# Two groups of three score banks for ScalarE with the third lent to VectorE, and one ring of 24 exp tiles

## Chip, cores and metric

The kernel runs on one core of a Trainium2 chip. The metric is the device time of one execution in microseconds, as the median of several runs; the profile is of one further execution. The profile's engines are PE (TensorE), PEld (its weight loads), ACT (ScalarE), DVE (VectorE), POOL (GpSimd) and SP (the engine that issues most DMAs).

## What is computed

Two independent halves whose outputs stand side by side in the last dimension: an SSM convolution (A) and an attention with 32 query heads on one shared key and value head (B). Everything is bf16 outside; S = 2048, D = 640, head size 20.

```python
# A: diagonal complex state space
Lam_bar = exp(dt * Lam);  B_bar = ((Lam_bar - 1) / Lam)[:, None] * Bmat
Bu = einsum("bld,pd->blp", x + 0j, B_bar)
h_t = Lam_bar * h_{t-1} + Bu_t
y = 2 * einsum("blp,dp->bld", h, Cmat).real + x * Dskip
# B: attention, 32 query heads on one key and one value head
q = (x @ wq) as 32 heads of 20;  k = x @ wk;  v = x @ wv
p = softmax(q k^T * 20 ** -0.5);  o = (p v) @ wo
out = concatenate([y, o], -1)
```

## The kernel before

**Work.** The attention is cut into 32 blocks (4 stretches of 512 queries, 8 groups of 4 heads). A block has 64 score tiles of 128 keys by 512 queries (16 key chunks, 4 heads), so there are 2048 in all. A score tile is one TensorE matmul into a PSUM bank (`score`, L1131). Its exponential is made in one of two ways:

- by ScalarE, for a *group* of adjacent banks at once: one ACTIVATE with Exp reads the group from PSUM (SC) and writes bf16 tiles to PR (L1117);
- by VectorE, for one tile: a TENSOR_SCALAR from its bank into an integer tile DR (`fill_d`, L1236), whose bits read as bf16 are an approximate exponential. It is sharpened by three shifted copies, made from DR to DR by VectorE in ones or pairs (`copy_source`) or by GpSimd in pairs (`pool_source`), each with its own scaled values VS. So one such tile needs four PV matmuls.

PV matmuls multiply exp tiles by the values and accumulate, four heads at a time, in one bank (`pv_source`, L1336). When all 64 tiles of a block are in, VectorE evacuates this bank (pvsb, L1385), and later steps divide by the sums and project with WO. SSM work (20 units of 10 VectorE steps or more, and 20 output steps), the query projections and the output projections are *tasks*: each takes a free bank from `misc` when its due number of tiles has been reached (`manager`).

**PSUM.** The 8 banks are: two exp groups, SC0 with three banks and SC1 with two (`CHUNKS`), two `misc` banks, and one bank for PV. VectorE's score tiles take a free misc bank.

**Exp buffers.** PR has 8 places (`NPS`), each of three tiles. Exp number k takes place k mod 8, and may not start before the PV matmuls of the last user of this place are done (the gate at L1120).

**Order.** The order of each engine's instructions is fixed when the program is built. A planner (`Schedule`, L40) keeps a model of the five engines with a duration for each step, and at each moment gives a free engine the ready step of the least `prio`. The steps that matter here: a group's fill 0, a block's PV evacuation 0.3, VectorE score tiles 0.5, SSM products out of PSUM 0.52, the other SSM steps 3, PV matmuls 2.0, or 0.9 when an exp place that is needed is still unread (`tight`). SSM steps that are late get 0.4 and a little, one step in each PAUSE. Semaphore waits are then derived from reads and writes. On the chip each engine does its instructions in this order, and each waits for the others.

**The fill.** `attention` alternates between the groups. A fill (`fill`, L1094) is one TensorE step: it scores the group's tiles, and up to `4 - n` VectorE tiles into free misc banks. It waits for the exp that last read the group. `want_d` and `can_d` decide on VectorE tiles: a share of at most 0.25, four of the 18 DR buffers free, a free bank.

Of the kernel before, what the change touches and what calls it, by code (L numbers as in the profile page):

```python
# [9 lines left out]
ALU = mybir.AluOpType  # L10
# [29 lines left out]
class Schedule:  # L40
# [12 lines left out]

    PAUSE = 1000.0
    LOCK = 60.0
# [102 lines left out]
    def pick(self, eng):  # L158
        urgent = None
        t = self.t  # L160
        cands = self.pending[eng]
        for src in self.sources[eng]:
            extra = src()
            if extra is not None:
                cands = cands + [extra]
        can, held = [], []
        for op in cands:
            r = self.ready(op)
            if r is None:
                continue  # L170
            if op.gate is not None and not op.gate():
                if op.due is not None and r <= t + 1e-6 and (urgent is None or op.due < urgent):
                    urgent = op.due
                continue
            if r <= t + 1e-6:
                if op.port:
                    if self.port_free["pool" if eng == "dve" else "dve"] > t + 1e-6:
                        if eng == "dve":
                            held.append(op)
                        continue  # L180
                    if eng == "pool" and self.port_wanted:
                        continue
                can.append(op)
            elif op.prio <= self.URGENT and (urgent is None or r < urgent):
                urgent = r
        best = key = None
        for op in can:
            p, dur = op.prio, op.dur
            if op.late and t >= self.late_from:
                p = 0.4 + 0.02 * p  # L190
            if eng == "pe" and op.mode != self.mode:
                dur += self.SWITCH
                if p > self.URGENT and self.stay():
                    p += self.STAY
            if urgent is not None and p > self.URGENT and t + dur > urgent + self.slack.get(eng, 1e9):
                continue
            if best is None or (p, op.seq) < key:
                best, key = op, (p, op.seq)
        if eng == "dve":
            self.port_wanted = any(best is None or op.prio < best.prio for op in held)  # L200
        return best
# [185 lines left out]
class Holder:  # L387


    def __init__(self, index):  # L390
        self.index = index
        self.left = 0
        self.users = []
        self.taken = False
        self.waits = False

# [10 lines left out]
class Build:  # L407
    CHUNKS = (3, 2)
    MISC = 2
    NPS = 8  # L410
    NOP = 7
# [58 lines left out]
    def alloc(self, o):  # L470
# [15 lines left out]
        self.WOt = sb(o, "WOt", [128, 640], BF16)  # L486
        self.PR = sb(o, "PR", [128, self.NPS, max(self.CHUNKS), 512], BF16)
        self.tab = sb(o, "tab", [128, 2, NC, 512], BF16)
# [114 lines left out]
    def program(self):  # L603
# [9 lines left out]
        self.state_op = {}  # L613
        self.hold = [Holder(i) for i in range(self.NPS)]
        self.nhold = 0
        self.dhold = [Holder(i) for i in range(self.NDS)]
# [26 lines left out]
    def warm_source(self):  # L643

        if self.started or self.s.t > 40000.0:
            return None
        p = self
        return Op("pe", [self.mm(self.pvbank.ap, p.PR[:, 0, 0, 0:128], p.PR[:, 0, 0, :], True, True)], 260.0, prio=9,
                  load=512.0, deps=[self.zero_op], reads=["PR0"], writes=[self.pvbank.key], hook=self.warm_last)
# [26 lines left out]
    def constants(self):  # L676
        self.zero_op = self.dve(lambda e: e.memset(self.PR[:, 0, 0, :], 0.0), 200, writes=["PR0"], prio=0.1)
        p = self
# [238 lines left out]
    def qt_task(self, bank):  # L917

        p = self
        prev = self.pe(self.four(bank, [p.VZ[:]] * 4, p.PR[:, 0, 0, :], True, False), self.mmt(512),  # L920
                       deps=[self.c_op["VZ"], self.zero_op] + bank.last, prio=0.95, mode="C", reads=["VZ", "PR0"], writes=[bank.key])
# [110 lines left out]
    def attention(self):  # L1032
# [8 lines left out]
        self.slot_last = [[op for b in bs for op in b.last] for _, bs in self.slots]  # L1041
        self.pv_gate = list(self.pvbank.last)
        while self.tile_n < NTILE:
            i = k % len(self.slots)
            yield lambda: (fill is None or fill.start is not None) and all(o.start is not None
                                                                          for o in self.slot_last[i])
            if self.tile_n >= NTILE:
                break
            n = min(self.CHUNKS[i], NTILE - self.tile_n)
            near = [self.act_block()]  # L1050
# [13 lines left out]
        for i in (k % 2, (k + 1) % 2):  # L1064
            yield lambda: fill.start is not None and all(o.start is not None for o in self.slot_last[i])
            for bank in self.slots[i][1]:
                bank.last, bank.busy = list(self.slot_last[i]), False
                self.misc.append(bank)
                self.free_banks.append(bank)

    MARGIN = 650.0

    def fill_now(self, op, i, n):

        s = self.s
        other = self.slot_last[1 - i]
        if len(other) != 1 or other[0].start is None or not self.d_count:
            return True
# [15 lines left out]
    def fill(self, op, i):  # L1094
        p = self
        t, banks = self.slots[i]
        n = min(self.CHUNKS[i], NTILE - self.tile_n)
        h = self.hold[self.nhold % self.NPS]
        self.nhold += 1
        extra, used = [], set()  # L1100
        while len(extra) < 4 - n and self.want_d(len(extra)):
            m = self.take_d(used)
            if m is None:
                break
            extra.append(m)
        tiles = [self.take_tile(used) for _ in range(n)]
        ents = []
        for x, m in enumerate(tiles):
            b, kc, j = self.score(op, m, t[:, 512 * x:512 * x + 512], banks[x])
            ents.append((b, kc, j, p.PR[:, h.index, x, :]))  # L1110
        for m in extra:
# [3 lines left out]
        op.load = 128.0 * len(op.fns)  # L1115
        dst = p.PR[:, h.index, 0:n, :]
        ex = self.act(lambda e: e.activation(dst, t[:, 0:512 * n], ACT.Exp, scale=1.0 / UNIT),  # L1117
                      0.8333 * 512 * n + 64, table="exp",
                      deps=[op], reads=[b.key for b in banks[:n]], writes=[f"PR{h.index}"], prio=0.5,
                      gate=lambda: not h.taken or (h.left == 0 and self.s.done(h.users)))  # L1120

        def on_start(_):
            h.taken, h.left, h.users, h.waits = True, n, [], False
        h.waits = True
        ex.hook = on_start
        self.slot_last[i] = [ex]
        for b, kc, j, rhs in ents:
            self.pvq[b][j].append((p.VP[:, kc, 0:32], kc, rhs, f"PR{h.index}", ex, h, "VP"))
            self.pv_filled[b] += 1

    def score(self, op, m, out, bank):  # L1131
# [65 lines left out]

    def want_d(self, taken=0):
        s = self.s
        if self.tile_n >= NTILE - 8 or self.d_count + taken + 1 > self.SHARE * (self.tile_n - 16):  # L1200
            return False
        if len(self.d_banks()) <= taken:
            return False
        return len(self.d_free()) > taken + len(self.SHIFTS) - 1

# [12 lines left out]
    ALONE, TASK, PV = 1.9, 0.95, 2.0  # L1218
    EV, P1, COPY, COPY1 = 0.52, 0.5, 0.56, 0.6
    CLOSE, PVEV = 0.3, 0.3  # L1220

# [13 lines left out]

    def fill_d(self, op, m):  # L1236

        p = self
        bank = self.d_banks()[0]
        self.take([bank])  # L1240
        h = self.d_free()[0]
# [5 lines left out]
        first = self.dve(self.ts(p.DR[:, h.index, :], bank.ap, 16256.0, 0.0, ALU.add, ALU.max), 663, deps=[op],  # L1247
                         reads=[bank.key], writes=[key], prio=self.P1)
        self.s.spawn(self.d_give(bank, first))
        self.d_open.append([h, first, list(range(1, n)), b, kc, j])  # L1250
        self.d_left[b, j] += n - 1
        self.pv_entry(b, kc, j, 0, h, first)
        self.pv_filled[b] += 1

    def pv_entry(self, b, kc, j, k, h, op):
# [80 lines left out]
    def pv_source(self):  # L1336
# [18 lines left out]
        left = sum(len(x) for x in q)  # L1355
        h = self.hold[self.nhold % self.NPS]
        tight = h.taken and h.left > 0 or any(x.waits and x.left > 0 for x in self.hold)
        if len(group) < 4 and not tight and not (complete and left < 12 and len(group) == sum(1 for x in q if x)):
            return None
        prio = 0.9 if tight else self.PV  # L1360
        return Op("pe", [], self.mmt(512, len(group)), prio=prio, mode="C", load=128.0 * len(group), hook=lambda op: self.pv(op, b, group))
# [166 lines left out]
    def finish(self, prev, rows, bank, ops, end=None):  # L1528
# [7 lines left out]
        else:  # L1536
            key, st = f"PR{end}", self.PR[:, end, 0, :]
        last = self.stage_dma.get(key)
# [13 lines left out]
    def ssm_scalars(self):  # L1552
# [128 lines left out]
        for c in range(NC):  # L1681
            self.diag_op = self.dve(self.ts(p.diagD[:, c, :], p.ident[:], sc[:, DSK, c:c + 1], None, ALU.mult), 160,
                                    deps=[sc_op, self.c_op["ident"]], reads=["sc", "ident"], writes=["diagD"], prio=3)
# [271 lines left out]
```

## Time and profile before

| | us |
|---|---|
| median of 5 runs | 768.7 (768.47 to 769.35) |
| profiled execution: whole, span | 769.16, 767.4 |
| ScalarE, VectorE, TensorE, GpSimd busy | 743.0, 666.4, 717.6, 436.4 |
| exps: first start, end of the last | 23.8, 755.8 |

In a group's row of the profile, the columns are the line, engine, operation, output and input tile with shapes, count, then busy us and the mean ns of one, then the idle time before them with what ended it. Buffer numbers are left out, so all PR places read PR, the two exp groups SC, and misc and PV banks MB. [...] A row of waits reads: who waited for whom, us in total, times, the longest. L581, L585, L595 and L600 are helpers that many steps share, so tiles tell them apart: SC<-QT,KT or MB<-QT,KT is a score, MB<-PR,VP and MB<-DR,VS are PV, MB<-xaT,BT and MB<-CT are SSM, DR<-MB is a VectorE score tile, DR<-DR its copies.

### The profile page before, as it was taken

To read this page: it belongs to the slowest core of one execution; us is meant where nothing else is said; L and a number is where in the kernel's file an instruction comes from. 1 tells how busy PE (TensorE), PEld (TensorE's weight loads), DVE (VectorE), ACT (ScalarE), POOL (GpSimd) and SP (SyncE) were. 2 spreads that over 40 slices of the span, in tenths; PEclk is the share of its full clock that TensorE was granted. 3 is DMA by queue.
4 is the path that set the end of the run, shared out by engine and by line. 5 is a ranking of instruction groups with operands and counts; after the bars stand their busy time and mean duration, and the time that the engine had idled before them with its cause. 6 is when DMAs were issued, how large, how long until landed. Compare 5 with 4: busy or idle time off the path is not lost.

```text
span 767.4 us, 24010 instructions
## 1 busy us (share of the span) xinstructions
PE 717.6 (94%) x10217; PEld 239.2 (31%) x10217; DVE 666.4 (87%) x1239; ACT 743.0 (97%) x668; POOL 436.4 (57%) x454
## 2 busy tenths in 40 slices
PE   9999999998999999999889999999989999999997
PEld 3432223222223233332233322223322332233223
DVE  6989999889899898999899888998988889984786
ACT  5899999999999999999999999999999999999994
POOL 4765666365556444466646575446556556556961
PEclk9999999999999999999999999999999999999999
DMA  9935200100001111020001111120000000001001
GB/s 192 137 89 100 62 24 8 41 20 9 9 18 25 31 30 57 30 48 14 7 12 32 35 31 34 46 50 17 11 18 15 25 25 22 16 11 28 25 10 42
DMA packets 61770, 27.87 MB, mean 36 GB/s; under 512 B 44936, under 2 KB 61664, under 8 KB 61664
## 3 DMA queue, kind: packets, MB, share of 16 engines
q1 hardware_dynamic: 60332, 26.20, 14.6%
q8 instruction: 81, 1.33, 0.7%
q10 hardware_dynamic: 1332, 0.13, 0.2%
q14 instruction: 25, 0.20, 0.1%
HBM read 8.31 MB, written 8.12 MB: 21 GB/s over the span
## 4 chain that ended last, share of the span: by engine, by line
ACT 81%; PE 15%; DVE 2%; SPq 1%; issue 0%; DMA 0%; POOL 0%; DVEq 0%; POOLq 0%
ACT PR L1117 81%; PE MB L581 5%; PE MB L585 5%; PE SC L585 4%; PE SC L581 1%; SPq L570 0%; DMA xaT<-in_A_x_dram 0%; POOL fr L600 0%; DVE QP L956 0%; DVE mab L814 0%; DVE fr L600 0%; DVE DR L600 0%; ACT tab L1622 0%; DVE prod L599 0%; DVE QT L600 0%
## 5 line engine op out<-in xcount | busy, mean ns | idle before, releaser
L1117 ACT ACTIVATE PR<-SC 128x1536 bf16<-128x1536 f32 (+1 forms) x642 | 726.6, 1374 | 5.6 <-PE MB L585 3.3
L595 POOL TENSOR_TENSOR DR<-DR,step 128x512 int32<-128x512 int32 x406 | 415.4, 1047 | 299.9 <-DVE DR L600 146.2
L600 DVE TENSOR_SCALAR DR<-MB 128x512 int16<-128x512 f32 x444 | 295.7, 684 | 64.2 <-PE MB L585 59.1
L585 PE MATMUL SC<-QT,KT 32*128 32x512 bf16 x1604 | 250.5, 384 | 40.0 <-ACT PR L1117 30.2
L585 PE MATMUL MB<-DR,VS 128*32 128x512 bf16 x1776 | 233.4, 384 | 0.4 <-DVE pvsb L1385 0.2
L585 PE MATMUL MB<-PR,VP 128*32 128x512 bf16 x1604 | 220.3, 385 | 0.9 <-DVE pvsb L1385 0.6
L585 PE MATMUL MB<-QT,KT 32*128 32x512 bf16 x444 | 160.3, 384 | 0.4 <-DVE prod L595 0.3
L585 PEld LDWEIGHTS SC<-QT,KT 32*128 32x128 bf16 x1604 | 63.8, 91 | 265.8 <-ACT PR L1117 181.4
L600 DVE TENSOR_SCALAR DR<-DR 128x1024 int16<-128x1024 int16 (+1 forms) x290 | 102.7, 408 | 7.8 <-PE MB L585 6.6
L585 PEld LDWEIGHTS MB<-DR,VS 128*32 128x32 bf16 x1776 | 59.4, 94 | 66.1 <-issue 38.1
L585 PEld LDWEIGHTS MB<-PR,VP 128*32 128x32 bf16 x1604 | 55.9, 94 | 63.2 <-issue 42.9
L581 PE MATMUL MB<-xaT,BT 128*32 128x512 bf16 x800 | 59.3, 382 | 0.3
L595 DVE TENSOR_TENSOR prod<-MB,Z 128x1024 bf16<-128x1024 f32 x40 | 48.6, 1215 | 4.8 <-PE MB L581 4.3
L585 PE MATMUL MB<-KT,VZ 128*32 128x256 bf16 x876 | 48.5, 275 | 0.0
L585 PEld LDWEIGHTS MB<-QT,KT 32*128 32x128 bf16 x444 | 38.1, 91 | 24.1 <-issue 14.8
L1725 DVE TENSOR_TENSOR_SCAN g<-sc,hst,u 128x512 bf16<-128x512 f32 x30 | 39.6, 1326 | 0.0
L595 DVE TENSOR_TENSOR prod<-g,tab 128x1024 bf16<-128x1024 bf16 x40 | 31.4, 786 | 0.0
L581 PE MATMUL MB<-xbT,wqf 128*32 128x512 bf16 x400 | 29.9, 395 | 0.5 <-DVE DR L600 0.2
L581 PE MATMUL MB<-CT,W 128*32 128x512 bf16 (+1 forms) x640 | 29.4, 301 | 0.2 <-DVE DR L600 0.2
L581 PE MATMUL MB<-CT,xbT 128*32 128x512 bf16 (+1 forms) x640 | 28.4, 301 | 0.1
L1542 DVE CAST stg<-MB 128x512 bf16<-128x512 f32 x35 | 24.0, 685 | 5.1 <-PE MB L581 4.7
L581 PE MATMUL MB<-WO,OP 128*32 128x128 bf16 (+1 forms) x580 | 27.1, 293 | 0.2
(137 smaller groups left out, 364.7 us busy)
## 6 DMA issues: line engine op xcount, KB each, us to landing
out_dram<-stg SPq DMA_DIRECT2D x35, 128.0 KB, 1.8
qd<-QP SPq DMA_DIRECT2D x20, 128.0 KB, 1.7
QT<-qd SPq DMA_DIRECT2D x28, 80.0 KB
OP<-pvsb SPq DMA_DIRECT2D x108, 20.0 KB
rdP<-recs SPq DMA_DIRECT2D x108, 20.0 KB
CT<-in_B_x_dram SPq DMA_DIRECT2D x2, 640.0 KB, 5.8
WO<-in_B_wo_dram SPq DMA_DIRECT2D x1, 800.0 KB, 4.7
wqf<-in_B_wq_dram SPq DMA_DIRECT2D x1, 700.0 KB, 5.9
```

Of the source, the lines that this page charges most:

```text
L581: r = e.matmul(out[32 * j:32 * j + 32], lhsT=lhsT[:, 32 * j:32 * j + 32], rhs=rhs, start=start, stop=stop, tile_position=(0, 32 * j), skip ...
L585: return lambda e: e.matmul(out, lhsT=lhsT, rhs=rhs, start=start, stop=stop, **kw)
L595: return lambda e: e.tensor_tensor(out, a, b, op)
L600: return lambda e: e.tensor_scalar(out, a, s1, s2, op0=op0, op1=op1)
L1117: ex = self.act(lambda e: e.activation(dst, t[:, 0:512 * n], ACT.Exp, scale=1.0 / UNIT), 0.8333 * 512 * n + 64, table="exp", deps=[op], re ...
L1542: ev = self.dve(lambda e: e.tensor_copy(st, bank.ap), 620, deps=[prev], reads=[bank.key], writes=[key], prio=self.EV, gate=(lambda: last.e ...
L1725: o = self.dve(lambda e, ri=ri, init=init: e.tensor_tensor_scan(p.g[:, u, ri, :], rdec, p.u[:, ri, :], init, ALU.mult, ALU.add), 1280, por ...
```

## The change

- Both exp groups have three banks, and one misc bank is left. The third banks are lent to `misc` until the first half of the queries is ready (`reclaim`); until then groups are of two tiles.
- In a fill of three, the third bank may hold a VectorE score tile (`want_own`). The exp then covers two tiles, VectorE evacuates the third, and the next fill of the group waits for both. Such a step has priority 0.42 and a due time. VectorE steps without a due time are not started when they would run past the earliest one.
- PR is one ring of 24 tiles, and an exp of two takes two. An exp waits for the PV matmuls of those whose tiles it takes.
- VectorE score tiles are not taken while an SSM unit is over 120 tiles late (`behind`).
- PV matmuls of a complete block have priority 0.9. PAUSE is 500 instead of 1000. One small VectorE step on the diagonal is marked as using the port shared with GpSimd.

```diff
-    PAUSE = 1000.0
+    PAUSE = 500.0
...
+        limit = min((op.due for op in self.pending[eng] if op.due is not None), default=1e18) if eng == "dve" else 1e18
         for op in can:
             p, dur = op.prio, op.dur
+            if op.due is None and t + dur > limit:
+                continue
...
-    CHUNKS = (3, 2)
-    MISC = 2
-    NPS = 8
+    CHUNKS = (3, 3)
+    MISC = 1
+    NPT = 24
...
     def attention(self):
...
+        self.cap = [n - 1 for n in self.CHUNKS]
+        for i in range(len(self.slots)):
+            lent = self.slots[i][1][-1]
+            self.misc.append(lent)
+            self.free_banks.append(lent)
+        s.spawn(self.reclaim())
...
     def fill(self, op, i):
-        n = min(self.CHUNKS[i], NTILE - self.tile_n)
-        h = self.hold[self.nhold % self.NPS]
-        self.nhold += 1
-        extra, used = [], set()
-        while len(extra) < 4 - n and self.want_d(len(extra)):
+        n = min(self.cap[i], NTILE - self.tile_n)
+        extra, used, own = [], set(), None
+        if n == 3 and self.want_own():
+            own = self.take_d(used)
+        if own is not None:
+            n = 2
+        while len(extra) < 4 - self.cap[i] and self.want_d(len(extra), own is not None):
...
         tiles = [self.take_tile(used) for _ in range(n)]
+        h = self.pr_take(n)
...
+        first = [] if own is None else [self.fill_d(op, own, banks[2])]
+        if first:
+            other = self.slot_last[1 - i][0]
+            begin = self.s.t + self.mmt(512, 4) + 200
+            if other.eng == "act":
+                begin = max(begin, other.start + other.dur if other.start is not None else self.s.t + other.dur)
+            first[0].due = begin + 2 * (0.8333 * 1024 + 64) - self.REFILL
...
-                      gate=lambda: not h.taken or (h.left == 0 and self.s.done(h.users)))
+                      gate=lambda: all(x.taken and x.left == 0 and self.s.done(x.users) for x in h.prev))
...
-        self.slot_last[i] = [ex]
+        self.slot_last[i] = [ex] + first
...
+    def reclaim(self):
+        yield lambda: (0, 0) in self.half_op
+        for i in range(len(self.slots)):
+            bank = self.slots[i][1][-1]
+            yield lambda: bank in self.free_banks
+            self.free_banks.remove(bank)
+            self.misc.remove(bank)
+            self.slot_last[i] = self.slot_last[i] + bank.last
+            self.cap[i] = self.CHUNKS[i]
...
+    def pr_next(self, n):
+        return self.pr_at if self.pr_at + n <= self.NPT else 0
+
+    def tight(self):
+        at = self.pr_next(3)
+        return any(x is not None and x.taken and x.left for x in self.owner[at:at + 3]) \
+            or any(x.left for h in self.waiting for x in h.prev)
+
+    WAITING = 2
+    REFILL = 900.0
+
+    def want_own(self):
+        if self.tile_n >= NTILE - 8 or self.d_count + 1 > self.SHARE * (self.tile_n - 16) or self.behind():
+            return False
+        if sum(1 for o in self.firsts if o.start is None) >= self.WAITING:
+            return False
+        self.firsts = [o for o in self.firsts if o.start is None]
+        return len(self.d_free()) > len(self.SHIFTS) - 1
...
+    def behind(self):
+        while self.next_unit < NQB * NC:
+            w = self.w_op.get(divmod(self.next_unit, NC))
+            if w is None or w.start is None:
+                return self.tile_n > self.unit_due[divmod(self.next_unit, NC)] + self.LAG
+            self.next_unit += 1
+        return False
...
     def want_d(self, taken=0, own=0):
...
-        if len(self.d_banks()) <= taken:
+        if len(self.d_banks()) <= taken or self.behind():
...
     def fill_d(self, op, m, bank=None):
+        own = bank is not None
+        if not own:
+            bank = self.d_banks()[0]
+            self.take([bank])
...
-                         reads=[bank.key], writes=[key], prio=self.P1)
-        self.s.spawn(self.d_give(bank, first))
+                         reads=[bank.key], writes=[key], prio=self.P1OWN if own else self.P1)
+        if own:
+            self.firsts.append(first)
+        else:
+            self.s.spawn(self.d_give(bank, first))
...
     def pv_source(self):
-        prio = 0.9 if tight else self.PV
+        prio = 0.9 if tight or complete else self.PV
```

## The prediction

> **What bounds the kernel now.** I read the page's busy shares first, then the chain that ended last, then the groups with shapes kept apart, then ScalarE's own waits and timeline.
>
> ```profile
> PE 717.6 (94%) x10217; PEld 239.2 (31%) x10217; DVE 666.4 (87%) x1239; ACT 743.0 (97%) x668; POOL 436.4 (57%) x454
> ```
> ```profile
> ACT 81%; PE 15%; DVE 2%; SPq 1%; issue 0%; DMA 0%; POOL 0%; DVEq 0%; POOLq 0%
> ```
> ScalarE (ACT) is busy 97% of the span and carries 81% of the chain. TensorE's 94% is no second bound: 876 of its matmuls (MB<-KT,VZ) are fillers issued only when the planner finds it underused. VectorE (DVE) at 87% is the one to watch.
>
> ```profile
> L1117 ACT ACTIVATE PR<-SC 128x1536 bf16<-128x1536 f32 x321 | 509.2, 1586 | 4.0 <-PE MB L585 1.9 <-PE SC L585 1.7
> L1117 ACT ACTIVATE PR<-SC 128x1024 bf16<-128x1024 f32 x320 | 371.8, 1162 | 1.6 <-PE MB L585 1.4
> L600 DVE TENSOR_SCALAR DR<-MB 128x512 int16<-128x512 f32 x444 | 295.7, 684 | 64.2 <-PE MB L585 59.1 <-POOL DR L595 0.2
> ```
> The exps (PR<-SC) are 321 of three tiles and 320 of two; VectorE makes 444 score tiles. The 1586 and 1162 ns overlap the next record: in the trace the middle distance from one exp's start to the next is 1335 ns for three tiles and 906 ns for two, so 429 ns for a tile and 48 ns for each instruction. A VectorE score tile costs 607 ns in the same measure. The exps run from 23.8 us to 755.8 us, 732 us; 321 x 1.335 + 320 x 0.906 + 0.5 for a last single tile are 718.9. Most of the remainder, 14.5 us over all pairs of starts (the rest is the last record's tail), is ScalarE waiting. Two waits stand out:
>
> ```profile
> ACT PR L1117 <- PE MB L585: 3.3, 2, 1.9
> ```
> ```profile
> 328.76 3.75 ACT L1117 ACTIVATE PR<-SC 128x1536 bf16<-128x1536 f32 x3
> 333.89 2.37 ACT L1117 ACTIVATE PR<-SC 128x1024 bf16<-128x1024 f32 x2 [1.37 <-PE MB L585]
> ```
> Here an exp waits not for scores but for a PV matmul (MB<-PR) to free its place in the exp ring. The other waits are late fills, many under 0.3 us. TensorE's weight loads say what a fill waits for:
>
> ```profile
> PEld SC L585 <- ACT PR L1117: 181.4, 410, 1.2
> PEld SC L585 <- DVE DR L600: 44.5, 100, 1.3
> ```
> A fill mostly waits for the exp that frees its banks, but 100 times for a VectorE score tile. The trace gives the loop's slack: a fill can start about 300 ns after the start of the exp running meanwhile, and an exp that came late started 442 ns after its fill. 742 of 906 ns: 164 ns are left.
>
> **The exps.** The changed kernel as built (its instruction order, without times) has 253 exps of three tiles and 414 of two: 1587 tiles against 1604, and 667 instructions against 642. 253 x 1.335 + 414 x 0.906 = 712.9 us against 718.9: **-6.0**. So 17 tiles (7.3 us) go to VectorE, and 25 more instructions at 48 ns give 1.2 us back. [...] The rows show 48 ns back to back, so I keep -6.0.
>
> **The ring.** It held 8 groups, a place of three tiles each: 8 x 1.12 = 9.0 us of exps. Now 24 tiles in a row: 24/2.38 groups x 1.069 = 10.8 us. It is 1.8 us deeper, the waits were 1.37 and 1.90 us, and the PV matmuls of a complete block move up to priority 0.9. I take **-3.2**. Ends: -3.6 (both, by start distances) and 0, if new ones come, since the last PV matmuls of a block still wait for the PV bank's evacuation. Behind the waiting exp stand all later exps; with the wait gone, its fill, already in place, lets it start.
>
> **A VectorE tile in the third bank.** 397 of 461 VectorE score tiles now sit in a ScalarE group (DR<-SC), only 64 elsewhere. The refill of that group then waits for the exp and for this VectorE instruction; queued behind it on TensorE are all PV, SSM and projection matmuls, and ScalarE waits one exp later. In the built order 139 fills name a VectorE instruction issued after the exp as a wait, against 68 before. How much room is there? A score tile's evacuation started at best 430 ns after its fill's start, and a fill that waited for one started about 730 ns after it. With exps of 906 ns the refill is due by 1812 + 164 ns after the last fill of that group, so an evacuation can be 1976 - 730 - 430 = 816 ns late for nothing.
>
> Own tiles come in 74 runs of 1 to 15 on successive two-tile exps. Within the runs I added up the VectorE order with the trace's start distances (score tile 607, pair copy 356, single copy 202, SSM product out of PSUM 1133, scan 1230, casts 600). Between two own tiles stand on average 312 ns of other work, so VectorE is asked for 919 ns per 906 ns exp: full, with no reserve, while over the whole kernel its order sums to 643 us against 622 before. Where the sum runs ahead of the exps by more than 816 ns, the excess is a stall: 7.6 us in 27 runs, or 5.0 without the first five, where which exps have an own tile is least sure. I take 6.3. It replaces 2.5 us of waits of exps behind VectorE score tiles in the old trace (20 late exps). Net **+3.8**. Ends: -2.5 (none stalls, excluded below that because no more of the kind existed) and +18.2 (VectorE 7% slower than the distances, as its 666.4 busy us stand to 622, and only 600 ns of room: 20.7 - 2.5).
>
> **Shorter windows.** Outside the large waits an exp of two lost 15 ns on average to late fills, one of three 7.6 ns. 414 and 253 of them make 8.1 us against 7.3; two thirds of that is not VectorE's: **+0.6**, ends 0 and +3.
>
> **What I cost at nothing.** Holding VectorE tiles back while SSM is late, PAUSE and the diagonal's port flag move VectorE and TensorE work that lies under exps; uncovered, it would show as SSM running past the last exp. In the built order the last SSM output stands 87 score matmuls before the end (91 before), some 30 us, so the cover holds. One misc bank fewer is made up by lending the two third banks until the first query half is ready. No DMA is added, 550 on SP's queue as before; GpSimd's copies go from 406 to 402. The head has the same ScalarE steps in nearly the same order; the first exps are of two tiles, and the start and the end (11.6 us after the last exp, outputs and their DMAs) may each move by 1 us.
>
> **Sum.** -6.0 - 3.2 + 3.8 + 0.6 = -4.8 us. The profiled execution took 769.16 us (span 767.4, 1.8 around it), 0.46 above the median of 768.7. So 764.4 for such an execution, and **763.9 us** as the median.
>
> **Rivals.**
> - *VectorE becomes the bound inside the runs (slower).* For it: 919 ns asked per 906 ns, and a static order, so one 1.2 us product in front of an own tile delays refill and exp. Against it: old own distances are 607 ns where the planner reckons 663, so it leaves slack, and it lets no undated VectorE step start that would overrun a dated score tile. With VectorE 7% slower the stalls are 13.6 us, and 20.7 with 600 ns of room; less 2.5 and with the other terms the kernel ends at 771 to 778, say 774 us. It decides from 11.1 us of such stalls on, 28 ns per own tile.
> - *The exps' gain is given back in full.* Ring waits return, since 1.8 us of depth is about the size of one wait, and own tiles stall by 6.3 us: -6.0 + 3.8 + 0.6 + 1 for the head, about 768.1 us.
> - *The larger gain.* Own tiles never stall, as their due times keep VectorE free: -6.0 - 3.6 - 2.5 = -12.1, less 1 for the end, about 755.6 to 757.5 us.
> - *It does not do what it says* is excluded for the counts: own tiles, the ring and the exps of two are in the built order.
>
> **Chances.** Likeliest, at 763.9 (761 to 767): 0.42. Larger gain, about 757: 0.16. Given back, about 768: 0.14. VectorE-bound, about 774: 0.28. The range of 8 in 10 runs from 756 to 775. About 0.2%, 1.5 us, is what measurement can tell from no change: faster 0.58, same 0.13, slower 0.29.
>
> **What would show it.** Right: two exp groups of 253 and 414, starts 1335 and 906 ns apart; ScalarE's wait for MB matmuls with PR gone or below 0.5 us; ScalarE's idle gaps small, and "SC <- DVE DR" among TensorE's waits above 44.5 us without ScalarE idling more than 10 us. Wrong: rows of ScalarE waiting for SC matmuls, released in turn by DVE DR<-SC, of 10 us or more in the runs of two-tile exps; VectorE busy over 700 us; or a start of the exps after 25 us.

## The result and the profile after

The changed kernel takes 765.85 us (median of 41 runs, 761.77 to 771.96), the kernel before 769.2 us beside it (76 runs, 768.09 to 770.97). The ratio is 0.9961 with a 95% interval of 0.9952 to 0.9970: 3.3 us faster. The prediction was 763.9, that is 4.8 us faster. A second difference was not forecast: the runs of the changed kernel lie 10 us apart, those of the kernel before 3 us.

The profiled execution took 767.64 us (span 765.9). Busy times of the page, then the chain that ended last:

```profile
PE 700.4 (91%) x10231; PEld 232.8 (30%) x10231; DVE 678.7 (89%) x1282; ACT 739.3 (97%) x693; POOL 431.4 (56%) x450
```
```profile
ACT 80%; PE 17%; DVE 1%; issue 1%; DMA 0%; POOL 0%; SPq 0%; DVEq 0%; POOLq 0%
```
ScalarE is still the bound: 97% busy, 80% of the chain. It has 3.7 us less work; VectorE has 12.3 us more, and stays under 700.

The groups with shapes kept apart:

```profile
L1139 ACT ACTIVATE PR<-SC 128x1024 bf16<-128x1024 f32 x414 | 399.1, 1124 | 7.3 <-PE SC L588 5.6 <-PE MB L588 1.0
L1139 ACT ACTIVATE PR<-SC 128x1536 bf16<-128x1536 f32 x253 | 355.1, 1573 | 0.5 <-PE SC L588 0.2
L603 DVE TENSOR_SCALAR DR<-SC 128x512 int16<-128x512 f32 x397 | 264.9, 684 | 37.6 <-PE SC L588 26.3 <-PE MB L588 8.5
```
The counts are those of the built program. In the trace the middle distances between starts are 1330 ns for three tiles and 904 for two, in the kernel before 1331 and 904; the 1335 and 906 of the prediction are a few ns high in both. So the exps alone are about 6 us shorter. The 397 new evacuations of a third bank take what an evacuation of a shared bank took, 684 ns.

ScalarE's waits and TensorE's weight loads that waited:

```profile
ACT PR L1139 <- PE SC L588: 5.8, 12, 1.8
ACT PR L1139 <- PE MB L588: 1.0, 1, 1.0
...
PEld SC L588 <- ACT PR L1139: 195.8, 415, 1.2
...
PEld SC L588 <- DVE DR L603: 51.9, 115, 0.9
```
The two ring waits of 3.3 us have become one of 1.0, and it is a score matmul, not a PV matmul of PR, that releases it. The loads wait 115 times for a VectorE score tile where it was 100, and none of these waits is longer than 0.9 us. What is new is the first row: 5.8 us of exps that wait for scores. The timeline of ScalarE shows where:

```profile
23.69 2.83 ACT L1139 ACTIVATE PR<-SC 128x1024 bf16<-128x1024 f32 x3
28.35 1.02 ACT L1139 ACTIVATE PR<-SC 128x1024 bf16<-128x1024 f32 x1 [1.83 <-PE SC L588]
30.29 1.02 ACT L1139 ACTIVATE PR<-SC 128x1024 bf16<-128x1024 f32 x1 [0.92 <-PE SC L588]
31.80 1.02 ACT L1139 ACTIVATE PR<-SC 128x1024 bf16<-128x1024 f32 x1 [0.49 <-PE SC L588]
33.31 1.02 ACT L1139 ACTIVATE PR<-SC 128x1024 bf16<-128x1024 f32 x1 [0.49 <-PE SC L588]
34.67 5.60 ACT L1139 ACTIVATE PR<-SC 128x1024 bf16<-128x1024 f32 x6 [0.33 <-PE SC L588]
```
Five exps in a row come late within 7 us of the head, 4.1 us in all. The view by stretches shows TensorE there. Its columns are stretch, length, busy us and instructions of TensorE, weight loads, VectorE, ScalarE and GpSimd, then the granted clock, the DMA share and GB/s. First the kernel before:

```profile
25.00:30.00 5.00, 4.69 (x112) 1.84 (x116) 4.76 (x12) 3.48 (x5) 4.51 (x10) 0.66 1.03 129
30.00:35.00 5.00, 4.83 (x67) 1.39 (x63) 4.66 (x10) 5.00 (x5) 4.28 (x10) 1.00 0.73 118
60.00:80.00 20.00, 18.41 (x229) 5.28 (x229) 17.95 (x35) 20.00 (x19) 11.06 (x12) 1.00 0.49 97
```
and the changed kernel:

```profile
25.00:30.00 5.00, 3.08 (x78) 1.10 (x76) 3.43 (x9) 2.54 (x3) 4.51 (x9) 0.70 0.55 92
30.00:35.00 5.00, 5.00 (x42) 1.08 (x40) 3.26 (x9) 3.40 (x4) 4.38 (x11) 0.62 0.23 59
60.00:80.00 20.00, 17.45 (x214) 5.23 (x214) 16.04 (x31) 19.86 (x19) 11.56 (x12) 0.95 0.54 98
```
Both have TensorE at half clock in the head, the kernel before for 3.4 us from 26.3 us on, the changed one for 6.8 us from 27.0 on, and again for 3.4 us at 78.2. From 30 to 35 us TensorE is busy all the time and finishes 42 matmuls where the kernel before finished 67. The stretch at 27.0 us has something in front of it: TensorE stands idle for 1.9 us in the midst of a row of small matmuls for v.

```profile
25.07 0.27 PE L584 MATMUL SC<-wvr,xbT 128*32 128x20 bf16 x15
27.25 0.52 PE L584 MATMUL SC<-wvr,xbT 128*32 128x20 bf16 x45 [1.92 <-issue]
```
"issue" means that the profile shows nothing that TensorE waited for. A gap among these matmuls that nothing shown ends, of 0.4 to 1.9 us, stands in the profiles of all kernels below with two groups of three, except own_light; the kernel before and the two kernels built on it have none. So it comes with the change, but not in every execution: own_light has the same TensorE order in the head, and its profile shows neither the gap nor a half-clock stretch. Its line for 25 to 30 us is

```profile
25.00:30.00 5.00, 5.00 (x116) 1.79 (x114) 4.79 (x14) 5.00 (x6) 4.43 (x10) 1.00 0.73 117
```

From the starts of the exps one can sum what ScalarE lost: each distance to the next exp that is over 40 ns beyond 1335 or 906 ns, sorted by what released the fill behind it. The table has the profiled executions that matter below, in us, with the number of late exps in brackets; the last four columns divide the loss after 40 us.

| kernel | first exp | lost before 40 us | lost after 40 us | behind PV of PR | behind a score tile in a shared bank | behind one in the third bank | behind anything else |
|---|---|---|---|---|---|---|---|
| before | 23.8 | 1.9 | 10.4 | 3.5 (6) | 4.2 (34) | none | 2.7 |
| changed | 23.7 | 4.6 | 13.4 | 0.2 (1) | 1.7 (4) | 5.5 (24) | 6.0 |
| own_light | 23.7 | 0.5 | 12.1 | 0.2 (1) | 1.7 (5) | 3.7 (26) | 6.5 |
| head_fill | 23.8 | 2.1 | 12.1 | 0.2 (1) | 1.5 (3) | 4.8 (24) | 5.6 |
| prod_light | 26.1 | 2.6 | 12.3 | 0.2 (1) | 1.4 (3) | 3.9 (17) | 6.8 |

Of these five, only the executions of the changed kernel and of prod_light have a half-clock stretch between 40 us and the last exp, each one of 3.4 us at 78 us.

Before to after: exps -6.0, losses in the head +2.7, losses later +3.0, distances late by 40 ns or less -0.7, first exp and tail -0.2. That is -1.2 against spans that differ by -1.5.

### The profile page after: what moved, and what is told of

The parts are those of the page before. It is cut to its first block, busy times and chain, and to the rows that moved or that the text cites. A ratio compares the mean times of both kernels' runs of the same rounds, so it can differ in the third digit from the quotient of the medians.

```text
span 765.9 us, 24175 instructions
## 1 busy us (share of the span) xinstructions
PE 700.4 (91%) x10231; PEld 232.8 (30%) x10231; DVE 678.7 (89%) x1282; ACT 739.3 (97%) x693; POOL 431.4 (56%) x450
## 4 chain that ended last, share of the span: by engine, by line
ACT 80%; PE 17%; DVE 1%; issue 1%; DMA 0%; POOL 0%; SPq 0%; DVEq 0%; POOLq 0%
ACT PR L1139 79%; PE MB L588 6%; PE SC L588 5%; PE MB L584 5%; PE SC L584 1%; DMA xaT<-in_A_x_dram 0%; ACT tab L1707 0%; POOL fr L603 0%; ACT PR L1625 0%; DVE fr L603 0%; DVE DR L603 0%; ACT L1713 0%; DVE prod L598 0%; DVE pvsb L1470 0%; DVE mab L818 0%
## 5 line engine op out<-in xcount | busy, mean ns | idle before, releaser
L1139 ACT ACTIVATE PR<-SC 128x1024 bf16<-128x1024 f32 (+1 forms) x667 | 723.0, 1295 | 7.8 <-PE SC L588 5.8
L598 POOL TENSOR_TENSOR DR<-DR,step 128x512 int32<-128x512 int32 x402 | 410.4, 1046 | 302.9 <-DVE DR L603 124.8
L588 PE MATMUL SC<-QT,KT 32*128 32x512 bf16 x1984 | 262.0, 386 | 51.5 <-ACT PR L1139 43.4
L603 DVE TENSOR_SCALAR DR<-SC 128x512 int16<-128x512 f32 x397 | 264.9, 684 | 37.6 <-PE SC L588 26.3
L588 PE MATMUL MB<-PR,VP 128*32 128x512 bf16 x1587 | 213.2, 385 | 1.7 <-ACT PR L1139 1.2
L588 PEld LDWEIGHTS SC<-QT,KT 32*128 32x128 bf16 x1984 | 67.8, 91 | 290.0 <-ACT PR L1139 195.8
L603 DVE TENSOR_SCALAR DR<-DR 128x1024 int16<-128x1024 int16 (+1 forms) x316 | 114.9, 417 | 12.8 <-PE MB L588 9.8
L603 DVE TENSOR_SCALAR DR<-MB 128x512 int16<-128x512 f32 x64 | 43.4, 679 | 2.5 <-PE MB L588 2.3
L1627 DVE CAST stg<-MB 128x512 bf16<-128x512 f32 x35 | 23.8, 679 | 5.3 <-PE MB L584 5.2
L588 PEld LDWEIGHTS MB<-KT,VZ 128*32 128x32 bf16 x840 | 21.4, 96 | 12.6 <-issue 6.2
L1470 DVE CAST pvsb<-MB 128x512 bf16<-128x512 f32 x32 | 21.8, 682 | 3.5 <-PE MB L588 3.3
```

The costliest lines, as they stand in the source:

```text
L588: return lambda e: e.matmul(out, lhsT=lhsT, rhs=rhs, start=start, stop=stop, **kw)
L598: return lambda e: e.tensor_tensor(out, a, b, op)
L603: return lambda e: e.tensor_scalar(out, a, s1, s2, op0=op0, op1=op1)
L1470: ev = self.dve(lambda e: e.tensor_copy(p.pvsb[:, slot, :], bank.ap), 620, deps=[op], reads=[bank.key], writes=[f"pvsb{slot}"], prio=self. ...
L1627: ev = self.dve(lambda e: e.tensor_copy(st, bank.ap), 620, deps=[prev], reads=[bank.key], writes=[key], prio=self.EV, gate=(lambda: last.e ...
```

## The experiments

Two theories of where 1.5 us of the forecast gain went. **VectorE** (A in the expectations): an own tile in the third bank is late because VectorE is full, as the prediction had it. **The clock** (B and C): TensorE falls to half clock after stretches with thin work, and fills come late. The second comes from the runs themselves: each run's record gives a mean granted clock. Over the 41 runs of the changed kernel it lies between 0.985 and 0.999, and a straight line through them falls by 0.66 us per 0.001. At 0.9975, about where the kernel before runs (0.997 or 0.998 in 60 of 64 runs, 0.994 to 0.996 in four), the line gives 763.7 us (within 0.5). The 11 runs at 0.997 or more have a median of 763.9 us. A stretch of 3.4 us at half clock takes 0.0022 off the mean, so 1.5 us by that line. The line alone is no proof: what holds up TensorE could lengthen a run and lower its clock at once. Below, "clock" is the mean over the runs of one kernel. The kernel before took 769.0 to 769.15 us beside each of these kernels.

**own_light.** VectorE's evacuation of an own tile at half size.

```diff
-        first = self.dve(self.ts(p.DR[:, h.index, :], bank.ap, 16256.0, 0.0, ALU.add, ALU.max), 663, deps=[op],
+        w = 256 if own else 512
+        first = self.dve(self.ts(p.DR[:, h.index, 0:w], bank.cols(0, w), 16256.0, 0.0, ALU.add, ALU.max), 663, deps=[op],
```


> The changed kernel with the same instruction order; the VectorE evacuation of a tile in an exp group covers 256 of 512 columns, so that part of the exponentials is left out. Each of the 397 takes some 267 ns less. Theory A (the refill waits for VectorE's own tile, some 5.5 us in the profile after): the changed kernel's 765.9 us falls by 4 to 5.5, to about 761, and the waits of fills for DVE DR<-SC nearly vanish. Rival B (what is given back is lost to stretches in which TensorE's clock is granted at half): it falls by less than 1 us, and the spread of 10 us between runs stays.

Measured: 765.91 us (762.49 to 768.53), ratio 0.9954 (0.9936 to 0.9973), clock 0.994. Nothing changed, though the row shows that the edit took hold:

```profile
L603 DVE TENSOR_SCALAR DR<-SC 128x256 int16<-128x256 f32 x393 | 163.5, 420 | 106.8 <-PE SC L588 87.7 <-PE MB L588 17.6
```
101 us less VectorE work (264.9 to 163.5) brought nothing, and idle time in front of these evacuations rose from 37.6 to 106.8 us. So that VectorE is full is not what costs the time; that theory falls. The exps behind a third bank lose 1.8 us less than in the changed kernel's profile, but no time comes of it; and 15 of the 26 late evacuations here begin after VectorE stood idle until their score came, so the fill was late and not VectorE. The line through these runs gives 763.6 at clock 0.9975, as for the changed kernel.

**keep_more.** More fillers for TensorE.

```diff
-    KEEP = 3500.0
+    KEEP = 5000.0
```


> The changed kernel with the planner's threshold for filler matmuls raised from 3500 to 5000: 2192 fillers in place of 840, exps of 710.7 us by their counts against 712.8. Rival B: the stretches at half clock go, some 1.9 us each and two to three in a mean run; with the exps' 2.1 us the time falls to about 760, and runs differ by less than 3 us. Theory A: only the exps' 2.1 us, 763.8, and the spread stays. If fillers get in the way of fills: over 766.

Measured: 770.63 us (767.67 to 774.62), ratio 1.0013 (0.9996 to 1.0031), clock 0.991. A miss for the clock: 2192 filler matmuls instead of 840 did not remove the half-clock stretches (10.2 us from 27.6 on, 6.8 us at 676). This source gives nothing before a PV block is open, and so nothing in the head. The time is that of the third case, fillers in the way of fills: the line through these runs gives 766.0 us at clock 0.9975 (within 1.2), 2.2 us above the changed kernel. The edit changes the order too, so it cannot tell what the stretches cost.

**ring_alone.** The kernel before with the ring of 24 tiles only.

```diff
-    NPS = 8
+    NPT = 24
...
-        h = self.hold[self.nhold % self.NPS]
-        self.nhold += 1
+        h = self.pr_take(n)
```


> The kernel before with one part of the change alone: the ring of 24 tiles in place of 8 places of three; groups of 3 and 2 as before. By counts the exps come to 720.7 us, 2.2 more than before. Theory A (the ring is worth the 3.6 us that ScalarE waited for it): 769.2 + 2.2 - 3.6 = 767.8, and no wait of an exp for PV matmuls. Rival (those waits move to other places): 771.4.

Measured: 769.8 us (768.81 to 770.97), ratio 1.0005 (0.9997 to 1.0014). This lies between the two cases. Its order has 322 and 321 exps and no single tile at the end, 720.7 us by counts against 718.9 with the single tile: 1.8 us more, not 2.2. So the ring itself gave about 1 us by the medians; in the profiles late exps behind PV of PR fell from 3.5 us (6) to 1.7 (2). Half of the waits stay.

**places_8.** The changed kernel with eight places of three tiles.

```diff
-        self.owner[at:at + n] = [h] * n
-        self.pr_at = at + n
+        self.owner[at:at + 3] = [h] * 3
+        self.pr_at = at + 3
```


> The changed kernel with the ring undone: each exp takes a place of three tiles, 8 places. Exps by counts 710.4 us against 712.8; depth 8 exps of 1.06 us, 8.5 us. Theory A: waits for the ring come back, 3.5 us or more, so 767 us or above. Rival (the ring gives nothing): 763.5.

Measured: 772.26 us (769.18 to 774.75), ratio 1.0036 (1.0022 to 1.0050), clock 0.988. 6.4 us more than the changed kernel, although its exps are 2.4 us shorter by counts: late exps behind PV of PR are back, 2.6 us (7), and part of the rest goes with the lower clock. At clock 0.9975 the line through its runs gives 768.1 us (within 1.5), 4.4 above the changed kernel. With two-tile exps the ring is worth more than in the kernel before, as far as a changed order allows the comparison.

**fill_small.** Each filler cut to one small matmul.

```diff
+        fns = [self.mm(bank.tensor[0:32, bank.off:bank.off + 16], p.VZ[:], p.KT[:, 0:16], False,
+                       False, tile_position=(0, 0), skip_group_check=True)]
         self.n_keep += 1
```


> The changed kernel with every filler cut down: where TensorE gets four 128-column matmuls that add zero to a PV bank while a window has nothing else for it, it now gets one of 16 columns. The order of the instructions on every engine is otherwise that of the changed kernel (252 + 415 three- and two-tile exps or within one of it), nothing of the computation is left out. Theory C (part of what the change should have brought is lost to TensorE's clock, which falls to half for stretches of 3.4 us after stretches with thin TensorE work): more such stretches than the two of the changed kernel's profile before 700 us, a mean granted clock under 0.985, and a median above the changed kernel's 765.9, by about 1.5 us for each stretch more: 768 to 780, with a wider spread. Rival (the fillers only stand in front of the next score tiles, and the clock is no matter): 764 to 766, the late exps released by a score matmul fewer than in the changed kernel.

The matmuls that go have 256 columns each, not 128.

Measured: 771.06 us (767.72 to 775.08), ratio 1.0032 (1.0011 to 1.0053), clock 0.979. 5.2 us slower by taking work away. Of the profile, by stretches:

```profile
120.00:140.00 20.00, 17.57 (x198) 5.57 (x198) 16.65 (x28) 19.33 (x18) 12.81 (x13) 0.91 0.12 32
140.00:160.00 20.00, 16.73 (x187) 5.15 (x179) 18.55 (x37) 18.97 (x18) 7.05 (x7) 0.91 0.04 10
160.00:180.00 20.00, 17.92 (x197) 5.19 (x194) 18.22 (x35) 19.36 (x19) 11.50 (x12) 0.91 0.03 6
```
and of the changed kernel:

```profile
120.00:140.00 20.00, 18.53 (x257) 6.13 (x250) 17.73 (x32) 20.00 (x19) 11.62 (x12) 1.00 0.11 30
140.00:160.00 20.00, 17.07 (x241) 5.61 (x233) 19.04 (x35) 19.93 (x19) 7.90 (x9) 1.00 0.04 11
160.00:180.00 20.00, 17.21 (x230) 5.35 (x222) 19.03 (x36) 19.61 (x19) 9.79 (x11) 1.00 0.05 10
```
Each stretch has 3.4 us at half clock where the changed kernel has none, and ScalarE is busy 57.7 of 60 us instead of 59.5. There are eight such stretches before the end, and ScalarE loses 19.8 us after 40 us instead of 13.4. Half clock is a cost here, and the fillers hold the clock up: its mean is 0.979 with the small fillers and 0.994 with the whole ones.

**head_fill.** Work for TensorE in the head, in the unused half of a bank.

```diff
+            if tb > 1:
+                prev.fns += [self.mm(bank.tensor[32 * j:32 * j + 32, bank.off + 256:bank.off + 512], p.VZ[:], p.KT[:, 0:256], True,
+                                     True, tile_position=(0, 32 * j), skip_group_check=True) for j in range(4)] * 2
```


> The changed kernel with more for TensorE to do in the head: behind each step of narrow v matmuls for token blocks 2 and 3, eight zero-weight matmuls of 256 columns in the same bank's unused half; the order of everything else is the same. Nothing of the computation is left out. Theory C: the half-clock stretch at 27 us goes or shrinks from 6.8 us to 3.4 or none, ScalarE's stall before 40 us (4.65 us in the changed kernel's profile, 1.9 in the kernel before's) falls to about 1.6, and the median is 762.5 to 764.5. Rival (the head is late because score tiles stand behind other work in TensorE's queue, not because of the clock): the added matmuls lengthen that queue, the stall grows, 766.5 to 768.

Measured: 763.98 us (763.54 to 765.75), ratio 0.9941 (0.9928 to 0.9954), clock 0.998. The head by stretches:

```profile
25.00:30.00 5.00, 4.45 (x135) 1.94 (x135) 3.76 (x12) 3.82 (x4) 4.49 (x9) 1.00 0.71 114
30.00:35.00 5.00, 5.00 (x65) 1.39 (x63) 4.86 (x13) 4.78 (x6) 4.46 (x10) 1.00 0.34 89
```
The half-clock stretch is gone, ScalarE loses 2.1 us before 40 us instead of 4.6, and the median is 1.9 us lower (the intervals of the two ratios just touch). Its five runs lie 2 us apart, the 41 of the changed kernel 10. No kernel here that computes the whole is faster.

**nolend.** No lending of the third banks at the start.

```diff
-        self.cap = [n - 1 for n in self.CHUNKS]
-        for i in range(len(self.slots)):
-            lent = self.slots[i][1][-1]
-            self.misc.append(lent)
-            self.free_banks.append(lent)
-        s.spawn(self.reclaim())
+        self.cap = list(self.CHUNKS)
```


> The changed kernel without the lending of the two third banks to the projections at the start: both groups are three banks from the first run on. By the counts of the program 262 three-tile and 399 two-tile exps (711.3 us at 1.335 and 0.906, 1.6 less than the changed kernel), but the projections have two banks fewer until then. Nothing of the computation is left out. Theory C (the head is worth what its stalls and clock cost): if the projections hold, the head's stall is like the kernel before's 1.9 us and the median is 762 to 764.5. Rival (the lending is what keeps the head going): stalls before 40 us above 6 us, 767 to 772.

Measured: 772.39 us (771.52 to 775.1), ratio 1.0053 (1.0037 to 1.0069), clock 0.987. In time this is the rival's side, but not in its place: the head loses 3.6 us, less than with lending. One exp at 54 us waits 4.3 us, and the half-clock stretches (6.8 us at 25 and at 565, 3.4 at 172) are more. The lending, with the order that the planner makes of it, pays beyond the head.

**nobehind.** VectorE tiles not held back for the SSM.

```diff
     def behind(self):
+        return False
...
```


> The changed kernel with the third part undone: VectorE score tiles are not held back while the SSM is late. By the counts of the program 222 three-tile and 442 two-tile exps (696.8 us at 1.335 and 0.906, 16 less than the changed kernel), because VectorE takes more of the tiles; but the last SSM output then comes after the last score tile instead of 87 tiles before it. Nothing of the computation is left out. If ScalarE's exps alone set the end: 750 to 755. If VectorE is then the engine that ends last (679 us busy in the changed kernel, and the tiles moved to it add about 70 x 0.67 = 47 us less what it idles): ScalarE ends early or is stalled between, VectorE is the largest part of the chain of waits, and 770 to 800. The prediction's rival of VectorE as the bound says the second.

Measured: 816.61 us (815.85 to 822.67), ratio 1.0643 (1.0610 to 1.0675). By stretches:

```profile
700.00:735.00 35.00, 30.08 (x456) 10.40 (x456) 32.75 (x71) 33.54 (x31) 16.34 (x16) 1.00 0.04 9
735.00:775.00 40.00, 33.62 (x816) 18.41 (x804) 33.15 (x51) 1.68 (x3) 1.04 (x1) 0.91 0.12 35
775.00:812.00 37.00, 15.19 (x392) 9.39 (x392) 24.21 (x36) 0.00 (x0) 0.00 (x0) 0.68 0.06 19
```
The last exp ends at 733.5 us, 21 us earlier than in the changed kernel, and then VectorE and TensorE work off the SSM for 80 us. The tail is longer than the 770 to 800 us expected for the whole allows.

**prod_light.** On top of head_fill, a shorter VectorE step in front of own tiles. In head_fill's trace each of the 24 late evacuations begins where another VectorE instruction ends, 10 of them (2.1 of 4.8 us; the expectation says 11) behind the product of a bank with Z, as here:

```profile
101.73 1.21 DVE L598 TENSOR_TENSOR prod<-MB,Z 128x1024 bf16<-128x1024 f32 x1
102.86 1.28 DVE L603 TENSOR_SCALAR DR<-SC 128x512 int16<-128x512 f32 x2
```
```diff
-        o = self.dve(self.tt(p.prod[:, ri, :, :], bc, zt, ALU.mult), 1135, deps=[prev, self.z_op[c]], prio=self.EV,
+        n = 256 if tb + c else 512
...
+        o = self.dve(self.tt(p.prod[:, ri, :, 0:n], bc, zt, ALU.mult), 1135, deps=[prev, self.z_op[c]], prio=self.EV,
```


> The kernel of head_fill (its clock holds still from run to run), with the longest of VectorE's SSM steps in front of which or behind which score tiles queue made shorter: the product of a PSUM bank with Z takes 256 of the 512 columns from the second unit on, so that half of each product is stale and the SSM output is wrong there; the order of the instructions on every engine is the same. In head_fill 24 late exps stand behind an evacuation of the third bank (4.8 us), and in every one of them the evacuation started at the end of another VectorE instruction, in 11 of the 24 of this product (1.21 us). Theory Q (what a VectorE tile in the third bank costs is the place in VectorE's in-order queue: the instruction in front of it): though only 40 instructions get shorter, by 0.6 us each, those 11 waits go, the row falls to about 2.5 us and the median by 1.5 to 2.5 us against head_fill, to 761.5 to 762.5. Rival (VectorE's total load sets it): 24 us less of 679 is 3.5%, a fifth of what was taken off in own_light, which did nothing: 763.5 to 764.5.

Measured: 764.73 us (763.61 to 767.2), ratio 0.9949 (0.9935 to 0.9964), clock 0.997. The waits behind the product went, as expected, and the number of late evacuations fell from 24 to 17; but the rest grew, and ScalarE loses 12.3 us after 40 us. This execution has a half-clock stretch at 78 us that head_fill's has not, and is the slowest of its six, so the two losses are not strictly alike; the medians show no gain either. Theory Q, as it was put, falls: taking such waits away does not bring their sum.

**before_head_fill.** The kernel before with the matmuls of head_fill.

> The kernel before with the same added matmuls in the head as in head_fill; the order of everything else is the kernel before's. Nothing of the computation is left out. The kernel before has one half-clock stretch of 3.4 us at 26 us and 1.9 us of ScalarE stall before 40 us. Theory C: that stretch goes too, and the median falls by 1.0 to 1.7 us to about 767.5; the change at an undisturbed clock is then 764.0 - 767.5 = -3.5 us. Rival (the stretch in the kernel before costs nothing, because it ends before ScalarE has caught up): 769.0, and the change at an undisturbed clock is -5, the exps' 6.0 less what the third bank's queue takes.

Measured: 769.16 us (768.63 to 770.45), ratio 1.0005 (0.9996 to 1.0014), clock 0.999. Its half-clock stretch went and nothing was gained: the rival's side. So the 1.5 us per stretch are no law. Whether the stretch costs nothing there is less sure: in the profile ScalarE loses 1.3 us before 40 us instead of 1.9, but the first exp starts at 24.8 us instead of 23.8, so the added matmuls may take what the clock gives. What this settles: with the head filled in both, the change is worth 763.98 - 769.16 = -5.2 us.

**no_own.** The groups of three for ScalarE alone.

```diff
-        if n == 3 and self.want_own():
+        if False:
```


> The changed kernel without VectorE's tiles in the third bank: the groups are three banks for ScalarE alone, and VectorE's tiles come from the shared banks only, of which the change leaves one besides the PV bank. Nothing of the computation is left out. By the counts of the program 567 three-tile and 21 two-tile exps (776.0 us at 1.335 and 0.906, 63 more than the changed kernel), because VectorE gets fewer tiles. If ScalarE sets the end then as now: 825 to 832, VectorE's busy time far under 679. If VectorE's tiles were what delays ScalarE by more than the counted exps, the stalls beyond the exps fall below 12 us and the time is under 825.

Measured: 826.62 us (823.16 to 831.25), ratio 1.0744 (1.0705 to 1.0783), clock 0.988. It follows the counts: VectorE 519.9 us busy, ScalarE 799.5. What ScalarE loses after 40 us is 11.3 us, about as in head_fill (12.1) with 397 own tiles. That own tiles add little to it is not shown by this: the profile has two half-clock stretches of 6.8 us, at 131 and 366 us, that head_fill's has not.

**best_try.** head_fill with a ring of 27, fillers also in a free shared bank, and the load of the small matmuls counted by the planner.

```diff
-    NPT = 24
+    NPT = 27
...
+        if not all((b, j) in self.pv_first for j in range(4)) or self.pv_filled[b] == 64 and sum(len(q) for q in self.pvq[b]) < 12:
+            free = self.d_banks()
+            if not free:
+                return None
+            bank = free[0]
```


> The kernel of head_fill with two more changes: fillers also into a free shared bank while the PV bank is closed (and TensorE's load counted for the narrow matmuls), and an exp ring of 27 tiles in place of 24. By the counts of the program 257 three-tile and 408 two-tile exps (712.7 us, as in head_fill). Nothing of the computation is left out. If the ring's waits (1.0 to 1.5 us in the changed kernel) are on the path and half-clock stretches still cost in some runs: 762 to 763.5. If both are spent already: 763.5 to 764.5.

Measured: 766.43 us (765.94 to 766.99), ratio 0.9968 (0.9956 to 0.9980), clock 0.998. A miss for both cases: 2.4 us slower than head_fill at the same clock. Its profile again has 3.4 us at half clock at 27 us and loses 3.0 us before 40 us. Which of the edits did it was not tried.

## Why the prediction was right, and where not

- **Exps, -6.0: right.** 253 and 414, at 1330 and 904 ns, the distances of the kernel before within 1 ns. These differ by 426 ns for a tile and leave 52 ns for an instruction, where the prediction had 429 and 48.
- **The ring, -3.2: right in size for the named wait.** Late exps behind PV of PR fell from 3.5 to 0.2 us; ring_alone and places_8 show that the ring does it, by 1 to 2 us alone and about 4 at an equal clock in the changed kernel.
- **VectorE's tile in the third bank, +3.8: the sum came near, the mechanism failed.** The rows show 5.5 us of late exps behind it and 2.5 us fewer behind tiles in shared banks (4.2 to 1.7), +3.0; with the head filled +2.1. But the step said why: "VectorE is asked for 919 ns per 906 ns exp: full, with no reserve". own_light took 101 us from VectorE and gained nothing, so fullness is not it. At one place or another an own tile meets an instruction in front of it, or its fill is itself late; prod_light removed the commonest instruction, and no time was gained. A row of waits names who was last, not what is gained without him.
- **Shorter windows, +0.6: too small.** Exps late behind anything else cost 2.7 us before and 6.0 after, 5.6 with the head filled: about +3. In the changed kernel's profile 3.2 us of it (16 exps) are fills that stand behind other work in TensorE's order, in the kernel before 0.1 (1); 1.9 us against 1.2 are fills that wait for an exp. This was not tried by itself.
- **"The start and the end may each move by 1 us", and no term for TensorE's clock: the step that failed.** The first exp starts when it did, but in the profiled execution the exps after it lose 2.7 us more: TensorE stands idle for 1.9 us at 25.3 us, and then runs at half clock. TensorE's work there is not less; own_light's execution does the same order with 116 matmuls and 5.00 us busy, at full clock, and loses 0.5 us. So the change brings this in some executions, by gaps of different length, and the median holds a part of it: head_fill, which keeps the clock up (0.998 against 0.994), is 1.9 us faster. That covers the 1.5 us between -3.3 and -4.8.
- **What was costed at nothing otherwise held, because its cover did:** nobehind shows the price without it, 51 us.
- The rival that VectorE becomes the bound needed 11.1 us of stalls behind own tiles; it got 5.5.

That the sum of -4.8 lies so near the -5.2 with the head filled is in part luck: there the third bank took 1.7 us less than forecast and the other late exps 2.3 us more. One reading in the prediction is off without consequence: 14.5 us of waiting cannot be most of a remainder of 732 - 718.9 = 13.1 us.

Open stays what sets the 10 to 12 us that ScalarE loses after 40 us in both kernels. Half evacuations, shorter products and no own tiles at all left it at 11 to 12 us. Open are also what holds TensorE up at 25 us, and whether the half-clock stretch of the kernel before costs anything. Not all of a run's time is the clock: in the profiled executions of the kernels above the first exp starts anywhere from 22.8 to 26.1 us. And fill_small shows both sides of a filler: the line through its own runs would give 761.1 us at clock 0.9975 (within 2), some 2.6 us under the changed kernel, but it never ran at such a clock (0.973 to 0.986).

## What to carry to other kernels

When the bounding engine's work is cut by counting instructions, ask also how steadily the engine that feeds it runs: here half-clock stretches of TensorE in part of the runs gave back over a third of the gain (1.9 of 5.2 us), and the prediction had no term for them. A larger spread between runs than before was a sign of it here (10 us against 3), and sorting the runs by their granted clock separated it without a further run (763.9 us for those at 0.997 or more, 765.85 for all). One profiled execution is one draw: what it loses in the head need not be lost in the next (4.6 us in the changed kernel's, 0.5 in own_light's with the same TensorE order there). Before trusting a row of waits as a gain, take the waited-for work away once: 101 us less VectorE work gained nothing here.

## What the hardware showed that was not expected

The granted TensorE clock moved in steps of 3.4 us between full and half: the stretches at half clock last 3.41 us (the kernel before at 26.3 us), 6.83 (the changed kernel at 27.0) and 10.24 (keep_more at 27.6). No long gap stands ahead of some of them: in the 3.4 us ahead of the changed kernel's stretch at 78.2 us TensorE's matmuls were busy 61% with no gap over 0.62 us, and ahead of the eight stretches of fill_small busy 55 to 76% with no gap over 0.79 us. The busy share alone does not mark them either: ahead of keep_more's stretch at 27.6 us, among small matmuls of 20 columns, it was 90%. What brings a stretch on stays open, and so does why it comes in one execution and not in another: own_light has the changed kernel's TensorE order in the head, and ran there at a clock of 1.00.
